# Moving k's turn one slot sooner and q's turn one slot later in a fused attention and expert kernel

## The chip, the cores and the metric

The kernel runs on one core of one Trainium2 chip. The metric is the device time in microseconds (us) of one execution. Four runs of the kernel before the change are shown, and one of them was profiled.

## The reference

Two stages are computed one after the other. The first is attention with a threshold, for 8 batches, 8 heads, 576 positions and head dimension 64. The second is a two-layer network over all 4608 rows, with a hidden width of 2048.

```
scores = (q @ k.T) / sqrt(64)
scores = where(scores >= rowmax(scores) - tau, scores, -1e9)     # tau = 0.02
attn   = exp(scores - rowmax);  attn /= rowsum(attn) + 1e-9
x      = (attn @ v), heads side by side                          # 4608 x 512
h      = x @ w_in                                                # 512 -> 2048
out    = (h - tanh(h)) @ w_out                                   # 2048 -> 512
```

Inputs and output are float32.

## The kernel before

**Tiles.** Two heads of one batch make a pair. There are 32 pairs, numbered 0 to 31, and four of them make a batch. A pair has 9 row tiles of 128 rows (`TPP`): tiles 0 to 3 are rows of the first head, tiles 5 to 8 of the second, and tile 4 ("M") holds the last 64 rows of both. There are 288 tiles in all.

**Slots.** One loop over `s` writes the order of all work by hand; each engine then executes its own instructions in that order. A step of this loop is called a slot here. In slot `s` the loop issues, in this order: `shift` (a small op on DVE that makes the bias `nb` from the row maxima) for tile s+7, `scores` for tile s+8 (`AHEAD` = 8), `kink` for tile s+5 (`MASK` = 5), `bend` (tanh on ACT of the hidden block of the slot before), `weights` of tile s (exp on ACT), one step of the two-layer network where there is one, `shrink` (DVE, `g`), stores, `attend` and `norm` for tiles of two slots before, `emit_x`, and at the end the steps that `plan` has for this slot. For pairs 0 to 3 `weights` and `attend` run four slots sooner.

**One tile.** `scores` (L327, and L317 for tile 4) multiplies qT with kT and with kS into one of two psum buffers of the pool `ps_big`. DVE copies this out with a scale and a row maximum (`sc`, L337), which frees the buffer. ACT masks it (`z`, L374). For pairs 0 to 5 PE transposes z (`psZ`, L394); from pair 6 on a DMA does it (`zT`, L382, on SP's queue). ACT takes the exponential (`pT`, L403 or L411), PE multiplies with v (`psO`, L440 and L429), and DVE normalises (L454, L455, L460). `emit_x` (L472, L478) transposes the result of a pair for the second stage.

**The second stage** of a batch is cut into steps of four matmuls: hidden steps (`psH`, L495, followed by tanh on ACT and `g` on DVE, L514) and output steps (`psY`, L521, followed by `yo` on DVE, L534). They are spread over slots of the following batch, beginning with its fifth slot, about one per slot.

**Preparing a pair.** Before pair p's first `scores` in slot `first` = 9p-8, these steps are put into `plan`:

```
PREP = ((LDK, load k), (LDK-1, load q), (LDK-2, load v),       # LDK = 16
        (8, split k), (7, split q), (5, turn k), (4, split_v))
```

A number d stands for slot `first` - d. `split` runs on POOL: three operations make a float16 high and low part (`khl` or `qhl`, L190 to L194). `turn` (L241) transposes nine 128x128 blocks on PE into a psum buffer of the same pool `ps_big` (`ps_k` or `ps_q`), and DVE copies them out (`kT` or `qT`, L264). For k, two copies on POOL then make `kS` (L270), with the halves exchanged. `split_v` runs on POOL after that. q's turn stands at d = 3, but for odd pairs from 9 on and for pair 30 (`q_by_dma`) it is a DMA transpose on SP's queue (L253) at d = 5. The weights are loaded in 16 pieces in the early slots, each followed by a cast on POOL (L628).

Since 9 slots make a pair, slot `first` - 5 is the slot in which the scores of the tile 4 of the pair before are issued.

Of the kernel before, what the change touches and what calls it, by code (L numbers as in the profile page):

```python
# [18 lines left out]
def kernel(  # L19
# [225 lines left out]
    def q_by_dma(p):  # L245

        return p >= 2 * HPAIR and (p % 2 == 1 or p == 30)

    def turn(p, t):
        hl = hls.pop((p, t))  # L250
        if t == "q" and q_by_dma(p):
            m = mats[p, t] = qk_pool.tile([P, W], FP16, name=f"{t}T", tag=t)
            nc.sync.dma_start_transpose(  # L253
                out=m.rearrange("p (c r) -> p c r", c=TPP),
                in_=hl.rearrange("p c a d -> p (c a d)"),
            )
            return
        ps = ps_big.tile([P, W], FP16, name=f"ps_{t}", tag="big")
        for c in range(TPP):
            turn_chunk(  # L260
                ps[:, c * P : (c + 1) * P], c, hl[:, c, :, :].rearrange("p a d -> p (a d)")
            )
        m = qk_pool.tile([P, W], FP16, name=f"{t}T", tag=t)
        nc.vector.tensor_copy(out=m, in_=ps)  # L264
        mats[p, t] = m
        if t == "k":
            sw = qk_pool.tile([P, W], FP16, name="kS", tag="ks")
            for lo, hi in ((0, D), (D, 0)):
                o, i = sw[lo : lo + D, :], m[hi : hi + D, :]
                nc.gpsimd.tensor_copy(out=o, in_=i)  # L270
            mats[p, "ks"] = sw
# [383 lines left out]
    for p in range(1, NPAIR):  # L655
        first = TPP * p - AHEAD
        for d, f in PREP[3 if p == 1 else 0 :]:
            d -= p == 1 and d in (3, 5)
            plan.setdefault(first - d, []).append(lambda p=p, f=f: f(p))
        d = 5 if q_by_dma(p) else 3 - (p == 1)  # L660
        plan.setdefault(first - d, []).append(lambda p=p: turn(p, "q"))

    load(0, "v")
# [27 lines left out]
    for s in range(-AHEAD, NTILE + LAG + 3):  # L691
        p, j = divmod(max(s, 0), TPP)
# [107 lines left out]
```

## Time and profile before

| what | value |
| --- | --- |
| median of four runs | 538.06 us (537.02 to 538.35) |
| the profiled execution | 538.18 us, of which the span of the instructions is 536.4 us |
| granted TensorE clock | 1.00 |
| busy: PE, DVE, ACT, POOL | 513.1, 427.4, 438.2, 290.9 us |
| scores copies `sc` on DVE (L337) | 288 of 0.752 us |
| k copies `kT` on DVE (L264) | 31 of 0.756 us |
| q copies `qT` on DVE (L264) | 18 of 0.752 us |
| `kS` copies on POOL (L270) | 62 of 1.143 us |
| q turns by DMA (L253) | 13, median 3.3 us from issue to landing |

PE is TensorE, DVE VectorE, ACT ScalarE, POOL GpSimd, and SP the queue that issues most DMAs. Matmuls are pipelined, so one that is listed with 0.379 us may be followed by the next much sooner, and a busy PE row is not PE at its peak. In the lines of the timeline the columns are: start, duration, engine, line, operation, output<-input, shapes and count, and in brackets the idle time before it with what ended it. The one who ended a wait is inferred, and where the engine named had long been done it was another.

### The profile page before, as it was taken

To read this page: it belongs to the slowest core of one execution; us is meant where nothing else is said; L and a number is where in the kernel's file an instruction comes from. 1 tells how busy PE (TensorE), PEld (TensorE's weight loads), DVE (VectorE), ACT (ScalarE), POOL (GpSimd) and SP (SyncE) were. 2 spreads that over 40 slices of the span, in tenths; PEclk is the share of its full clock that TensorE was granted. 3 is DMA by queue.
4 is the path that set the end of the run, shared out by engine and by line. 5 is a ranking of instruction groups with operands and counts; after the bars stand their busy time and mean duration, and the time that the engine had idled before them with its cause. 6 is when DMAs were issued, how large, how long until landed. Compare 5 with 4: busy or idle time off the path is not lost.

```text
span 536.4 us, 13042 instructions
## 1 busy us (share of the span) xinstructions
PE 513.1 (96%) x4782; PEld 287.9 (54%) x4782; DVE 427.4 (80%) x1202; ACT 438.2 (82%) x630; POOL 290.9 (54%) x390
## 2 busy tenths in 40 slices
PE   8989899998999999999999999999999999999997
PEld 4666565554555555555555555555555455444444
DVE  5889878988888988889888988898888888554440
ACT  5999888998898989899888989898989989543330
POOL 7999995766555666657555755566665720000000
PEclk9999999999999999999999999999999999999999
DMA  7555656998997988799988999889979885401113
GB/s 207 178 185 145 207 165 137 183 204 155 184 200 171 174 198 188 167 183 177 201 190 179 190 182 191 168 179 195 188 165 182 188 151 113 104 21 39 39 41 78
DMA packets 204768, 85.76 MB, mean 160 GB/s; under 512 B 172320, under 2 KB 197152, under 8 KB 204704
## 3 DMA queue, kind: packets, MB, share of 16 engines
q1 hardware_dynamic: 204112, 84.51, 73.8%
q8 instruction: 37, 0.61, 0.5%
q10 hardware_dynamic: 592, 0.43, 0.3%
q14 instruction: 27, 0.22, 0.1%
HBM read 36.70 MB, written 9.44 MB: 86 GB/s over the span
## 4 chain that ended last, share of the span: by engine, by line
PE 69%; DVE 16%; POOL 7%; ACT 3%; issue 3%; DMA 1%; SPq 0%; DVEq 0%; POOLq 0%; ACTq 0%
PE psY L521 21%; PE psH L495 18%; PE psS L327 14%; DVE sc L337 7%; PE psO L440 5%; DVE g L514 3%; PE psS L317 3%; PE psHt L495 3%; PE ps_k L241 2%; DVE kT L264 2%; ACT pT L403 2%; POOL kS L270 2%; DVE yo L534 1%; ACT z L374 1%; POOL w_in_sb L628 1%
## 5 line engine op out<-in xcount | busy, mean ns | idle before, releaser
L337 DVE TENSOR_SCALAR_CACHE_REDUCE sc<-psS 128x576 f32<-128x576 f32 x288 | 216.0, 752 | 23.2 <-PE psS L327 14.3
L374 ACT ACTIVATE z<-sc,nb 128x576 bf16<-128x576 f32 x256 | 193.5, 769 | 19.5 <-DVE nb L354 19.4
L521 PE MATMUL psY<-w_out_sb,g 128*128 128x512 bf16 (+1 forms) x592 | 146.0, 374 | 0.8 <-DVE yo L534 0.8
L411 ACT ACTIVATE pT<-zT 128x1152 f16<-128x1152 bf16 (+1 forms) x130 | 138.9, 1069 | 2.0 <-DMA zT<-z 2.0
L270 POOL COPY kS<-kT 64x1152 f16<-64x1152 f16 x62 | 70.8, 1143 | 128.2 <-DVE nb L354 126.6
L495 PE MATMUL psH<-xT,w_in_sb 128*128 128x512 bf16 x480 | 124.0, 379 | 2.3 <-DVE g L514 2.3
L327 PE MATMUL psS<-kT,qT 128*128 128x512 f16 (+1 forms) x512 | 104.4, 285 | 7.8 <-DVE sc L337 3.7
L508 ACT ACTIVATE th<-psH 128x512 f32<-128x512 f32 x128 | 75.5, 589 | 36.7 <-PE psH L495 35.5
L327 PEld LDWEIGHTS <-qT 128*128 128x128 f16 x1024 | 72.4, 97 | 57.8 <-issue 10.0
L514 DVE SCALAR_TENSOR_TENSOR g<-th,psH 128x512 bf16<-128x512 f32 x128 | 87.3, 682 | 18.7 <-ACT th L508 18.7
L327 PE MATMUL psS<-kS,qT 128*128 128x512 f16 x496 | 101.3, 286 | 0.9 <-POOL kS L270 0.7
L521 PEld LDWEIGHTS <-g 128*128 128x128 bf16 x592 | 50.7, 98 | 56.9 <-issue 4.0
L495 PEld LDWEIGHTS <-w_in_sb 128*128 128x128 bf16 x576 | 49.2, 98 | 58.2 <-issue 4.5
L440 PEld LDWEIGHTS <-pT 128*128 128x128 f16 x1280 | 55.7, 98 | 25.2 <-issue 1.9
L440 PE MATMUL psO<-vb,pT 128*128 128x65 bf16 x1280 | 61.2, 193 | 0.0
L194 POOL TENSOR_TENSOR khl<-kraw,khl 128x576 f16<-128x576 f32 x31 | 39.7, 1282 | 2.6
L194 POOL TENSOR_TENSOR qhl<-qraw,qhl 128x576 f16<-128x576 f32 x31 | 39.7, 1281 | 2.6
L403 ACT ACTIVATE pT<-psZ 128x640 f16<-128x640 bf16 (+1 forms) x54 | 35.5, 659 | 5.8 <-PE psZ L394 5.6
L264 DVE COPY kT<-ps_k 128x1152 f16<-128x1152 f16 x31 | 23.4, 756 | 14.1 <-PE ps_k L241 14.1
L534 DVE COPY yo<-psY 128x512 f32<-128x512 f32 (+1 forms) x31 | 21.1, 682 | 13.1 <-PE psY L521 11.1
L455 DVE TENSOR_TENSOR osb<-psO,rc 128x256 bf16<-128x256 f32 x64 | 27.2, 424 | 2.2
L354 DVE TENSOR_SCALAR nb<-mx 128x6 f32<-128x6 f32 (+1 forms) x160 | 24.4, 153 | 2.3
(81 smaller groups left out, 508.8 us busy)
## 6 DMA issues: line engine op xcount, KB each, us to landing
vraw<-in_v_dram SPq DMA_DIRECT2D x32, 256.0 KB, 3.5
out_dram<-yo SPq DMA_DIRECT2D x32, 256.0 KB, 2.8
kraw<-in_k_dram SPq DMA_DIRECT2D x31, 256.0 KB, 3.1
qraw<-in_q_dram SPq DMA_DIRECT2D x31, 256.0 KB, 3.7
wt<-in_moe_w_in_dram SPq DMA_DIRECT2D x8, 512.0 KB, 4.5
wt<-in_moe_w_out_dram SPq DMA_DIRECT2D x8, 512.0 KB, 4.6
zT<-z SPq DMA_TRANSPOSE x104, 3.5
kraw<-in_k_dram SPq DMA_DIRECT2D x32, 32.0 KB, 3.0
```

The lines of the kernel that those rows point to most:

```text
L194: nc.gpsimd.tensor_tensor(out=hl[:, :, 1, :], in0=x, in1=hl[:, :, 0, :], op=ALU.subtract)
L270: nc.gpsimd.tensor_copy(out=o, in_=i)
L327: nc.tensor.matmul(out=ps[:, dst], lhsT=lhs, rhs=kk[:, src], start=(n == 0), stop=(n == 1),)
L337: nc.vector.tensor_scalar(out=sc, in0=ps[:, lo : lo + S], scalar1=SC, scalar2=None, op0=ALU.mult, op1=ALU.max, accum_out=mx[:, c : c + 1],)
L374: nc.scalar.activation(out=z, in_=sc, func=ACT.Prelu, bias=nb, scale=1.0, alpha=STEEP)
L403: nc.scalar.activation(out=pt[:, off * P : (off + n) * P], in_=ps[:, 0 : n * P], func=ACT.Exp)
L411: nc.scalar.activation(out=pt[:, 0 : n * P], in_=zts.pop(i)[:, 0:n, :], func=ACT.Exp)
L440: nc.tensor.matmul(out=po[:, (j - 1 - 5 * hh) + ab, :], lhsT=pt[:, blk * P : (blk + 1) * P], rhs=vb[:, hh, c, :], start=(n == 0), stop=(n ...
L495: nc.tensor.matmul(out=ps, lhsT=w_in_sb[:, c, n * P : (n + 1) * P], rhs=xs[m][:, c, :] if m < B else xR[:, c, :, :], start=(c == 0), stop= ...
L508: nc.scalar.activation(out=th, in_=ps, func=ACT.Tanh)
L514: nc.vector.scalar_tensor_tensor(out=gs[m][:, n, :], in0=th, scalar=-1.0, in1=ps, op0=ALU.mult, op1=ALU.add,)
L521: nc.tensor.matmul(out=ps, lhsT=gs[m][:, n, ms * P : (ms + 1) * P], rhs=w_out_sb[:, n, cols], start=(n == 0), stop=(n == DF_C - 1),)
```

## The change

From pair 5 on, k's turn is put into slot `first` - 6 instead of `first` - 5. From pair 5 on, q's turn is put into slot `first` - 2 instead of `first` - 3 where PE does it; where a DMA does it (d = 5) it stays. Pair 4, the first of the second batch, and the pairs before it keep their slots. Nothing else is edited.

```diff
         for d, f in PREP[3 if p == 1 else 0 :]:
             d -= p == 1 and d in (3, 5)
+            if d == 5 and p >= 5:
+                d = 6
             plan.setdefault(first - d, []).append(lambda p=p, f=f: f(p))
-        d = 5 if q_by_dma(p) else 3 - (p == 1)
+        d = 5 if q_by_dma(p) else (2) if p >= 5 else 3 - (p == 1)
         plan.setdefault(first - d, []).append(lambda p=p: turn(p, "q"))
```

## The prediction

> **What bounds the kernel now.** I read the page's busy shares first, then busy time by stretch, then the waits of PE, then the order of events around the turns of single pairs. A slot is one step of the main loop. F stands for slot 9p-8, in which pair p's first score block is issued; F-6 is six slots earlier. Here are the page's busy line, and the stretches with their columns.
>
> ```profile
> PE 513.1 (96%) x4782; PEld 287.9 (54%) x4782; DVE 427.4 (80%) x1202; ACT 438.2 (82%) x630; POOL 290.9 (54%) x390
> ```
> ```profile
> core 0: us, PE busy (x) PEld busy (x) DVE busy (x) ACT busy (x) POOL busy (x), PEclk, DMA share, GB/s
> 55.00:78.00 23.00, 19.98 (x235) 13.05 (x234) 19.17 (x57) 19.55 (x32) 21.81 (x27) 1.00 0.56 181
> 78.00:94.00 16.00, 14.68 (x171) 9.56 (x169) 12.83 (x35) 13.98 (x24) 10.05 (x13) 1.00 0.69 150
> 107.40:135.00 27.60, 25.14 (x253) 14.25 (x252) 23.85 (x72) 25.03 (x35) 18.49 (x25) 1.00 0.90 182
> ...
> 165.60:223.60 58.00, 57.32 (x544) 31.91 (x543) 51.32 (x149) 52.33 (x73) 34.58 (x45) 1.00 0.85 184
> ```
>
> The last line is one batch of four pairs in the steady part: PE idles 0.68 us of 58. Four 512-column matmuls take 1.03 us and one alone 0.379, so each further one adds 0.217 us, and they follow one another at that step. The steady part is therefore bound by PE's own work, which the change doesn't alter. From 55 to 135 us it is different: PE idles 3.0, 1.3 and 2.5 us in the stretches shown, and POOL is busy for 21.8 of the first 23. This is where the moved turns can gain or lose.
>
> The Trainium skill (Perfetto Trace Analysis, Identifying the Most-Contended Engine) says that matmul busy time tells little about the distance to the roofline and that weight-load busy time and FLOPs should be used. By its 54% (287.9 us of 536.4) the steady part would look nearly half empty; the estimate by that page is that moved turns could shift the end by tens of us either way. Since the matmuls' starts already lie back to back, I go by the starts.
>
> ```profile
> PE psS L327 <- DVE sc L337: 3.7, 13, 0.8
> PE ps_q L241 <- POOL qhl L194: 1.9, 4, 1.0
> PE psZ L394 <- ACT pT L403: 1.3, 5, 0.3
> PE psS L327 <- DMA qT<-qhl: 1.2, 1, 1.2
> ```
>
> In PE's waits (total, times, longest), no turn costs more than a few us in the whole run. That caps the gain: the moves can't return more than the waits near them.
>
> **The change, part by part.** No instruction is added or removed. For 27 pairs (5 to 31) k's nine transposes (9 x 0.055 = 0.5 us of PE), its 0.756 us copy on DVE and its two 1.143 us copies on POOL are issued at the end of slot F-6 instead of F-5. For 14 pairs (5, 6, 7 and the even ones from 8 to 28) q's nine transposes and 0.752 us copy go from the end of F-3 to the end of F-2. The other q turns go by DMA and keep their place, so SP's order is unchanged. On POOL only one thing moves: in pair 5 the kS copies now precede a 1.04 us weight cast. The cast ends 2.4 us later, and SP's next weight load with pair 7's k load behind it waits for it (issued near 64.3 instead of 61.9). Pair 7's split starts at 77.4, so 10 us cover a 3.1 us load: nothing.
>
> *Pair 5.* POOL ends khl at 57.71.
>
> ```profile
> 56.58 0.48 PE L440 MATMUL psO<-vb,pT 128*128 128x65 bf16 x10
> 57.76 0.68 PE L241 MATMUL ps_k<-ident_f,khl 128*128 128x128 f16 x9
> 60.50 0.68 PE L241 MATMUL ps_q<-ident_f,qhl 128*128 128x128 f16 x9 [0.42 <-POOL qhl L194]
> 63.87 0.41 PE L327 MATMUL psS<-kS,qT 128*128 128x512 f16 x2 [0.30 <-POOL kS L270]
> ```
>
> Moved, k's turn stands right after that psO (issued out by 56.9) and waits until 57.76: 0.85 us in place of the 0.27 us that it waits now. The tile-4 scores queue behind it. The kT copy ends near 59.3 and F-4 needs its psum buffer: 59.34 for 58.63. q's turn no longer waits for qhl (0.59 us) but for sc of F-3, near 62.2; qT is ready near 63.7, just where F now waits for kS (ready near 62.8 instead). F's second half runs at 64.0 for 63.87. ACT, which is busy without a break from 64.6 to 71, starts its pT about 0.5 us later: I take +0.5 us, between 0 and +0.9 (the whole displacement of F-4 and more).
>
> *Pair 6.* khl ends at 68.93 and k's turn would be ready at 68.6 with pair 5's delay: it waits 0.4 us, but this swallows most of that delay. F-4 is late by 0.7. Then q's turn is gone from F-3, where F-2 now waits 0.43 us for DVE: F-2 runs at 74.4 for 74.88. F comes at 77.6 for 77.68. Net after pair 6: -0.1 us.
>
> *Pair 7.* khl is 3 us early. F-2 waits 0.82 us (90.77) because q's buffer waits behind norm, sc and g on DVE; moved, F-2 starts near 89.1. But q's turn then ends near 92.3, the qT copy near 93.1, and F needs it: 93.16 for 93.20. A gain of 1.7 us is given back at F. DVE keeps about 0.2 us of it.
>
> *Pairs 8 and 9.* DVE runs without a break from 101 to 112 us, and the same operations only change places: F-1's 0.46 us wait for the qT copy becomes a 0.35 us wait for sc. I take 0 for pair 8, and +0.1 for pair 9, whose tile-4 scores wait about 0.5 us for DVE in place of the 0.30 us at 116.42.
>
> *Pair 10* is the one real gain.
>
> ```profile
> 128.33 0.69 DVE L514 SCALAR_TENSOR_TENSOR g<-th,psH 128x512 bf16<-128x512 f32 x1 [1.22 <-ACT th L508]
> 128.93 0.75 DVE L264 COPY kT<-ps_k 128x1152 f16<-128x1152 f16 x1
> 129.73 0.41 PE L327 MATMUL psS<-kT,qT 128*128 128x512 f16 x2 [0.90 <-DVE nb L354]
> ```
>
> The kT copy is queued behind a g that waits 1.22 us for ACT's tanh, and F-3's scores wait for the buffer that this copy frees. Moved, the copy stands before that g and ends near 126.1; F-3 waits for sc only and starts near 128.7, 1.0 us earlier. F-2's 0.21 us wait goes too. What is late next: pair 11's qT by DMA. Pair 11's F (149.91) already waits 0.22 us for it, and SP issues it behind a zT that waits for ACT; ACT runs unbroken from 124.7 to 141.5 and comes forward by about 0.5 us only. I keep -0.5 (from 0 to -1.2).
>
> *The steady pairs, 11 to 31.* Cover, not gain, is what matters here. khl is ready 2 to 7 us before even the new place. Odd pairs: yo, then g, then the kT copy end 0.1 to 0.2 us before F-4 needs the buffer (pair 19: g ends 258.82, copy 259.57, F-4 issues at 259.72). Pairs 14, 18 and so on: k's turn fills PE until 358.59 (pair 26), and the tile-4 scores' buffer comes free at 358.58. q, even pairs: the turn ends about 0.17 us after its last start, the copy takes 0.75, and F comes 1.35 us (scores 0.49 plus a layer step 0.87) after the turn: a margin of 0.3 us. The nb of tiles 2 and 3 now stands behind the kT copy and ACT's z waits 0.7 to 0.9 us longer for it; ACT has idle time of 0.4 to 1.3 us just before or after (392.57: 0.78). I take 0, between -0.3 and +3 (below).
>
> The Trainium skill (Perfetto Trace Analysis, Optimization Strategy) says that a gap that repeats can mean too few buffers for the next tile. By that rule the two "big" buffers stay as scarce as they were, the moves cure nothing, and the sum is 0. The pair-10 rows show one gap that comes from queue order.
>
> Sum: +0.5 - 0.6 - 0.2 + 0.1 - 0.5 = -0.7 us, rounded to -0.6, since gains ahead of a resynchronising wait tend to be lost. The profiled execution took 538.18 us with a span of 536.4 (1.8 outside it, unchanged) and stands 0.12 above the median of 538.06. I forecast from the median: 537.5.
>
> **The rivals.** *Faster: the stalls between 56 and 135 us go for good.* The waits at the moved places, 0.59 (pair 5), 0.60 (6), 0.98 (7), 0.46 (8), 1.06 and 0.37 (10), are 4.1 us; less 1.4 for the new khl waits and their echo, 2.7 us remain: 535.4. For it: ACT and DVE have about 15% idle in these stretches. Against it: in pairs 5 and 7 F needs qT at once.
>
> *Slower: qT comes too late at F in the steady even pairs.* The margin is 0.3 us. A 0.60 us g between sc and the qT copy turns it into a wait of 0.3 us; over ten pairs (10, 12, ... 28) that is 3.0 us: 541.1. It decides once the copy starts over 0.3 us after the turn's end. Against it: in the changed order sc of F-2 stands directly before the qT copy in these pairs. For it: kT and qT copies now start 0.1 to 0.4 us after their turn, so margins of 0.1 to 0.3 are thin everywhere.
>
> *It does nothing to the steady part and the early terms cancel:* 538.1; this lies inside my forecast's range.
>
> **How the numbers follow.** This kernel's measurement tells about 0.2% (1.1 us) from no change. Within it, 0.43: the forecast's own range of 537.0 to 538.9 (pair 10 kept whole; pair 5 at its worst). Faster, 0.30: the first rival, or a part of it with pair 10 kept whole. Slower, 0.27: the second rival, or thin margins missed by 0.1 us in the 21 steady pairs (+2.1). The range for 8 in 10 is 535.6 to 540.4: nearly all of the faster case, and the slower one up to 2.3 us.
>
> **What would show it.** Right: ps_k waits for khl in pairs 5 and 6 of 0.4 to 0.9 us; the 1.06 us gap near 129.7 gone; PE busy in a steady batch still 57.3 of 58. Wrong: a wait of PE's scores for qT (or kT) that recurs in every even (or odd) pair, or a batch that is longer or shorter than 58.0 by over 0.2 us.

## The result: 0.2% faster, most of it in a part that was forecast to give nothing

The changed kernel takes 535.97 us (median of 36 runs, 534.62 to 537.04) against 537.12 us of the kernel before on the same chip (58 runs, 535.88 to 538.4). The ratio is 0.9977, with an interval of 0.9973 to 0.9982: by the ratio 1.24 us faster (1.0 to 1.5). That lies just over the 0.2% that count as a change here. The forecast was 537.5 us in a range of 535.6 to 540.4, with no change as the likeliest outcome. It was worked from 538.06 us, the median of the first four runs; 0.94 of the 1.53 us between forecast and measured time lie in the lower median that 58 runs give for the kernel before.

The two profiled executions are further apart: spans of 533.7 and 536.4 us. The profiled execution of before was one of its longer ones (538.18 us, 1.1 above the median just given), so the traces overstate the gain about twofold. They are used below for where things moved, and the times for how much it is worth.

From the page after, the busy line; and PE's busy time by stretch, with the columns of the table before (us, busy and instructions of each engine, clock, DMA share, GB/s):

```profile
PE 511.9 (96%) x4782; PEld 290.1 (54%) x4782; DVE 427.7 (80%) x1202; ACT 438.4 (82%) x630; POOL 291.0 (55%) x390
```
```profile
55.00:78.00 23.00, 19.50 (x233) 12.91 (x232) 18.91 (x56) 19.46 (x32) 21.75 (x28) 1.00 0.55 178
78.00:94.00 16.00, 15.05 (x171) 9.70 (x170) 13.62 (x40) 15.15 (x25) 9.95 (x12) 1.00 0.68 150
107.40:135.00 27.60, 25.29 (x256) 14.60 (x255) 24.11 (x74) 25.85 (x36) 19.94 (x26) 1.00 0.98 175
165.60:223.60 58.00, 57.41 (x548) 32.31 (x546) 51.57 (x147) 52.58 (x73) 34.78 (x45) 1.00 0.85 184
```

No engine does other work than before. Pair 5's stretch lost 0.5 us of PE's busy time, the next one won 0.4, the third (with pair 10) 0.15. The steady stretch shows 57.41 for 57.32, which looks like nothing. A busy share can't resolve what happened there; the starts of PE's instructions can. This table gives how much sooner (-) the first scores F of a pair start in the trace after than in the trace before, counted from pair 4, the last that the change doesn't touch:

| pair | 5 | 6 | 7 | 8 | 9 | 10 | 11 | 12 | 29 | 30 | end |
| --- | --- | --- | --- | --- | --- | --- | --- | --- | --- | --- | --- |
| us | +0.89 | +0.24 | +0.05 | -0.25 | +1.02 | -0.81 | -1.03 | -1.04 | -1.96 | -2.46 | -2.46 |

From pair 12 to pair 29, in the part forecast at 0, another 0.92 us is gained. It comes in equal steps of 0.21 us, at pairs 14, 18, 22 and 26 (the 0.09 at 27 is a wait of before for a qT by DMA): every steady batch takes 57.75 us instead of 57.96.

The waits of PE after, in total, times and longest:

```profile
PE psS L327 <- DVE sc L337: 2.4, 9, 0.4
PE psS L327 <- DMA qT<-qhl: 1.8, 2, 1.0
PE ps_q L241 <- POOL qhl L194: 1.5, 3, 1.0
...
PE ps_k L241 <- POOL khl L194: 0.7, 1, 0.7
```

The waits of the scores for `sc` fell from 3.7 to 2.4 us. The wait for a qT that a DMA brings rose from 1.2 to 1.8, and the forecast wait for khl is there once, in pair 5.

On the page the group of the kT copies points at DVE (busy, mean ns | idle of DVE just before, and what ended it). It is shown for before, then after:

```profile
L264 DVE COPY kT<-ps_k 128x1152 f16<-128x1152 f16 x31 | 23.4, 756 | 14.1 <-PE ps_k L241 14.1
```
```profile
L264 DVE COPY kT<-ps_k 128x1152 f16<-128x1152 f16 x31 | 23.4, 756 | 7.2 <-PE ps_k L241 6.8
```

DVE used to stand idle for 14.1 us in front of these copies, waiting for k's turn, and now only for 7.2 us. The row before was in the page that the forecast was made from, and the forecast does not use it. It is a pointer and not a price, since most of that idle time went to another place: in front of the qT copies it rose by about as much. The waits of DVE, before, then after:

```profile
DVE qT L264 <- PE ps_q L241: 0.7, 1, 0.7
```
```profile
DVE qT L264 <- PE ps_q L241: 7.3, 12, 0.7
```

What counts is which wait is passed on to PE.

### Where a steady batch wins 0.21 us

There are two places. The first is the joint of two batches, where for a few slots PE has no step of the second stage between two scores. Here it is before, around F of pair 25 (start, duration, engine, line, operation, tiles):

```profile
348.45 0.76 DVE L264 COPY kT<-ps_k 128x1152 f16<-128x1152 f16 x1 [1.09 <-PE ps_k L241]
...
353.04 0.68 DVE L514 SCALAR_TENSOR_TENSOR g<-th,psH 128x512 bf16<-128x512 f32 x1
...
353.34 0.41 PE L327 MATMUL psS<-kT,qT 128*128 128x512 f16 x2
...
353.64 0.75 DVE L337 TENSOR_SCALAR_CACHE_REDUCE sc<-psS 128x576 f32<-128x576 f32 x1
...
354.45 0.41 PE L327 MATMUL psS<-kT,qT 128*128 128x512 f16 x2
```

And after:

```profile
344.72 0.76 DVE L264 COPY kT<-ps_k 128x1152 f16<-128x1152 f16 x1
...
347.04 0.76 DVE L337 TENSOR_SCALAR_CACHE_REDUCE sc<-psS 128x576 f32<-128x576 f32 x1 [0.64 <-PE psS L327]
...
351.50 0.41 PE L327 MATMUL psS<-kT,qT 128*128 128x512 f16 x2
351.70 0.76 DVE L337 TENSOR_SCALAR_CACHE_REDUCE sc<-psS 128x576 f32<-128x576 f32 x1 [0.30 <-PE psS L327]
...
352.52 0.41 PE L327 MATMUL psS<-kT,qT 128*128 128x512 f16 x2
```

Before, DVE idles 1.09 us for k's turn and is then behind. The `sc` at 353.64 belongs to the scores before F and starts late, straight after the `g` at 353.04; the scores after F (354.45) need the buffer that it frees, and start 1.11 us after F (353.34). After, the kT copy (344.72) starts without a wait, and DVE is ahead: it waits for scores (0.64 us at 347.04), and the same `sc` (351.70) has waited 0.30 us for its scores, so it starts as soon as it can, and the distance is 1.02 us (351.50 to 352.52). That is 0.09 us.

The second place is q's turn in pairs 14, 18, 22 and 26. Before, in pair 26:

```profile
360.39 0.68 DVE L514 SCALAR_TENSOR_TENSOR g<-th,psH 128x512 bf16<-128x512 f32 x1
...
360.98 0.75 DVE L264 COPY kT<-ps_k 128x1152 f16<-128x1152 f16 x1
...
363.21 0.74 DVE L337 TENSOR_SCALAR_CACHE_REDUCE sc<-psS 128x576 f32<-128x576 f32 x1
...
363.40 0.67 PE L241 MATMUL ps_q<-ident_f,qhl 128*128 128x128 f16 x9
...
364.01 0.41 PE L327 MATMUL psS<-kT,qT 128*128 128x512 f16 x2
```

After:

```profile
363.14 0.67 PE L241 MATMUL ps_q<-ident_f,qhl 128*128 128x128 f16 x9
363.64 0.41 PE L327 MATMUL psS<-kT,qT 128*128 128x512 f16 x2
363.84 0.76 DVE L264 COPY qT<-ps_q 128x1152 f16<-128x1152 f16 x1 [0.60 <-PE ps_q L241]
...
364.99 0.41 PE L327 MATMUL psS<-kT,qT 128*128 128x512 f16 x2
```

Before, kT stood behind `yo` and `g`, DVE ran late, and the scores after q's turn started 0.61 us after it instead of 0.50: they waited 0.11 us for the buffer that the `sc` at 363.21 frees. After, the distance is 0.50. Both waits are shorter than a matmul is listed with (0.379 us), so they hide in the busy time of the row.

### The profile page after: what moved, and what is told of

Its sections match the earlier page's. It is cut to its first block, busy times and chain, and to the rows that moved or that the text cites. A ratio compares the mean times of both kernels' runs of the same rounds, so it can differ in the third digit from the quotient of the medians.

```text
span 533.7 us, 13053 instructions
## 1 busy us (share of the span) xinstructions
PE 511.9 (96%) x4782; PEld 290.1 (54%) x4782; DVE 427.7 (80%) x1202; ACT 438.4 (82%) x630; POOL 291.0 (55%) x390
## 4 chain that ended last, share of the span: by engine, by line
PE 75%; POOL 8%; DVE 6%; DMA 4%; ACT 3%; issue 2%; SPq 1%; POOLq 0%; DVEq 0%; ACTq 0%
PE psY L521 23%; PE psH L495 19%; PE psS L327 16%; PE psO L440 5%; PE psS L317 3%; DVE sc L337 3%; PE psHt L495 3%; PE ps_k L241 2%; POOL kS L270 2%; DMA qT<-qhl 2%; POOL w_in_sb L628 1%; PE psO L429 1%; PE ps_q L241 1%; DVE g L514 1%; DVE yo L534 1%
```

## The experiments

All are edits of the two lines that the change touches. The diffs of `k_only`, `q_only` and `dma_only` are taken against the kernel before, the others against the changed kernel, and they show only the lines that differ. Runs with a ratio were timed beside the kernel before on the same chip. In this table "steady" is the length of a steady batch in the trace, "F waits" the sum of what F waits for a qT by DMA over the odd pairs from 9 on and pair 30, and "pair 12" and "end" are shifts as in the table above.

| kernel | ratio | steady | F waits | pair 12 | end |
| --- | --- | --- | --- | --- | --- |
| before, and the profile again | | 57.96, 57.96 | 1.7, 2.1 | 0, +0.11 | 0, -0.16 |
| the change | 0.9977 [0.9973, 0.9982] | 57.75 | 2.1 | -1.04 | -2.46 |
| k_only | 0.9978 [0.9969, 0.9988] | 57.75 | 1.9 | -1.69 | -1.63 |
| q_only | 0.9964 [0.9952, 0.9977] | 57.86 | 1.9 | -1.80 | -2.80 |
| early_only | 1.0007 [0.9995, 1.0019] | 57.97 | 1.8 | -1.15 | -1.62 |
| late_only | 0.9982 [0.9973, 0.9992] | 57.75 | 2.2 | -0.72 | -0.99 |
| q_two | 1.0221 [1.0207, 1.0235] | 59.80 | 1.8 | +3.68 | +11.51 |
| qdma6 | 0.9938 [0.9924, 0.9951] | 57.75 | 0 | -1.82 | -4.22 |
| best | 0.9925 [0.9911, 0.9939] | 57.75 | 0 | -2.41 | -4.81 |
| dma_only | 0.9977 [0.9967, 0.9987] | 57.96 | 0 | -1.57 | -3.04 |
| early_dma | 0.9960 [0.9947, 0.9972] | 57.96 | 0 | -1.83 | -3.29 |

Single executions scatter: `late_only` is the kernel before up to F of pair 10, and its trace stands 0.48 us sooner there and 0.72 at pair 12 all the same. Shifts at pair 12 and at the end carry that uncertainty; the steady batch, which repeats within 0.01 us but for single waits such as that of `k_only` in pair 22, does not.

**k_only**: k's turn sooner, q's left in its place.

```diff
+            if d == 5 and p >= 5:
+                d = 6
```

> Only k's turn is moved (pairs 5 to 31); q's turn keeps its slot. Theory A (both moves gain by shortening waits in the steady part, 0.1 us a batch each, and k's also ends the wait in pair 10): a steady batch takes 57.88 us (before 57.98, both moves 57.75), the gap of about 1 us in pair 10 is gone, and the time is 0.9980 to 0.9988 of before. Theory B (all of the gain lies before 150 us, as the forecast had it): a steady batch takes 57.98 us and the time is 0.9985 to 0.9995. Theory C (the difference of the two profiles is mostly chance in when the q transposes by DMA land): the time is within 0.9995 to 1.0005.

Measured: 0.9978, with a steady batch of 57.75 us. k's move alone gives the whole step of 0.21 us, where half of it (57.88 us) had been expected. Its trace gives much of this back later in single waits: 0.52 us after q's turn in pair 22, and 0.76 and 1.15 us at F of pairs 27 and 30 for a qT by DMA.

**q_only**: q's turn later, k's left in its place.

```diff
-        d = 5 if q_by_dma(p) else 3 - (p == 1)
+        d = 5 if q_by_dma(p) else (2) if p >= 5 else 3 - (p == 1)
```

> Only q's turn is moved (pairs 5, 6, 7 and the even ones from 8 to 28); k's turn keeps its slot. Theory A: a steady batch takes 57.87 us (the 0.11 us wait of the scores after q's turn in pairs 14, 18 and so on is gone, the wait at the joint of two batches stays), the gap in pair 10 stays, and the time is 0.9985 to 0.9998 of before. Theory B: a steady batch takes 57.98 us, time 0.9995 to 1.0010. Theory C: the same as B.

Measured: 0.9964, with a steady batch of 57.86 us. q's move gives half of the step: with q later, the second place (q's turn in every fourth pair) has no wait, while the joint keeps its 1.11 us. The two moves overlap; they do not add (0.21 and 0.10, together 0.21).

The time is another matter: 0.9964 is 1.9 us (1.2 to 2.6), far beyond the 0.9985 to 0.9998 expected and no worse than the whole change (0.9977). The steady batches give 0.4 us of it. The rest lies elsewhere: in its trace F is 0.40 us sooner in pair 6, 0.75 in pair 8 and 1.80 in pair 12, and pair 10's gap, which was expected to stay, is gone. How much of that the edit causes was not settled, since a single execution scatters by 0.7 us there.

**early_only** and **late_only**: both moves, for pairs 5 to 10 only, and for pairs 11 and up only.

```diff
-            if d == 5 and p >= 5:
+            if d == 5 and 5 <= p <= 10:
```
```diff
-            if d == 5 and p >= 5:
+            if d == 5 and p >= 11:
```

(with the same condition in the line for q)

> Both turns are moved for pairs 5 to 10 only. Theory A: a steady batch takes 57.98 us, as before, and the time is 0.9985 to 0.9995 of before (pair 10's 1.0 us, less what pairs 5 and 6 lose to the wait for khl). Theory B: the whole gain, 0.9973 to 0.9982. Theory C: 0.9995 to 1.0010.

> Both turns are moved for pairs 11 to 31 only. Theory A: a steady batch takes 57.75 us and the time is 0.9975 to 0.9985 of before (0.2 us in each of five to six batches, and up to 0.4 us less wait for pair 30's q transpose). Theory B: a steady batch takes 57.98 us and the time is 0.9995 to 1.0005. Theory C: as B.

Measured: 1.0007 and 0.9982. The steady pairs carry the gain (0.97 us, between 0.4 and 1.5; the trace gives 0.92 between pairs 12 and 29, in `late_only` as in the changed kernel). `early_only` keeps the batch of before, and its time is that of the expectation by which the early gain is chance. The six early pairs with both moves, in which the forecast saw all that was to be won or lost, give nothing that the times show: between 0.3 us of gain and 1.0 us of loss. The one trace of `early_only` has pair 12 sooner by 1.15 us, but that execution took 536.31 us and was among the shortest of its kernel (median 537.61).

**before_2**: the kernel before, profiled once more.

> The kernel before once more, for a second profile. Theory C' (where the early waits fall is chance of one execution): pair 10's wait of 1.06 and 0.37 us and the F waits of pairs 9, 11, 27 and 30 come out differently by 0.5 us or more in all, while a steady batch takes 57.98 us again. If the pair-10 wait is fixed by the queue order, it is again 1.0 to 1.4 us.

Measured: 538.17 us. The gap in front of pair 10's F-3 is there again (0.91 us, before 1.06, and 0.37 in front of F-2 in both), as expected if the order of the queues makes it. The waits of F for a qT by DMA are not the same: 0.30, 0.51, 0.12, 0.46 and 0.71 us in pairs 9, 11, 25, 27 and 30, where the first trace has 0.22, 0.09 and 1.38 in pairs 11, 27 and 30. Those waits vary from one execution to the next by up to 0.7 us each, which is more than the effect of a steady batch.

**qdma6**: the change, with the DMA transposes of q issued one slot sooner.

```diff
-        d = 5 if q_by_dma(p) else (2) if p >= 5 else 3 - (p == 1)
+        d = 6 if q_by_dma(p) else (2) if p >= 5 else 3 - (p == 1)
```

> Both turns moved as in the change, and the q transposes by DMA (odd pairs from 9, pair 30) are issued one slot sooner too, in slot F-6. In the profiles so far the F scores of pairs 9, 11, 27 and 30 wait between 1.7 and 2.2 us in all for a transposed q. Theory D (these waits are what keeps the early gain out of the times): they fall under 0.8 us in all, a steady batch stays at 57.75 us, and the time is 0.9945 to 0.9965 of before. Theory E (SP's queue and the DMA engines are full there, so a sooner q transpose only delays the z transposes behind it): ACT's wait for zT grows by about what F's wait falls, and the time is 0.9970 to 0.9990.

Measured: 0.9938, a little better than the 0.9945 to 0.9965 expected, and F never waits for such a qT. ACT's wait for zT, which by the other theory would have grown, is 0.3 us in all (0.7 in the changed kernel). In pair 30 the changed kernel issues it and waits for it as follows:

```profile
419.00 1.56 SPq L253 DMA_TRANSPOSE qT<-qhl  x1
...
423.22 0.42 PE L327 MATMUL psS<-kT,qT 128*128 128x512 f16 x2 [0.82 <-DMA qT<-qhl]
```

In `qdma6` the same scores find it there:

```profile
414.38 1.64 SPq L253 DMA_TRANSPOSE qT<-qhl  x1
...
421.15 0.41 PE L327 MATMUL psS<-kT,qT 128*128 128x512 f16 x2
```

From issue to use it is 4.2 us in the first, with a wait, and 6.8 in the second, without one. The gain is more than the 1.6 us of one slot (57.75 us for 36), because on SP's queue the transpose now stands ahead of two loads of q, a zT and a store instead of behind them.

**q_two**: the change, with q's turn one slot later still.

```diff
-        d = 5 if q_by_dma(p) else (2) if p >= 5 else 3 - (p == 1)
+        d = 5 if q_by_dma(p) else (1) if p >= 5 else 3 - (p == 1)
```

> k's turn as in the change, q's turn two slots later than before, at the end of slot F-1, so that F's scores stand right behind it on PE. If the forecast's margin of 0.3 us (a layer step and scores, 1.35 us, less 0.17 us latency, 0.75 us copy and semaphores) is what hides the qT copy, then nothing hides it here: F waits about 1.0 us in each even pair, a steady batch takes about 59.8 us (57.75 plus two such waits) and the time is 1.014 to 1.022 of before. If PE had hidden slack, a batch would stay under 58.5 us and the time under 1.008.

Measured: 1.0221 and 59.80 us a batch, both as expected, the time at the edge of its range. This is the slower rival with its point passed: qT's copy comes after F is due, in every even pair. The chain of turn, copy and F in the trace of `q_two`, pair 26:

```profile
375.82 0.67 PE L241 MATMUL ps_q<-ident_f,qhl 128*128 128x128 f16 x9
...
376.53 0.76 DVE L264 COPY qT<-ps_q 128x1152 f16<-128x1152 f16 x1
377.34 0.42 PE L327 MATMUL psS<-kT,qT 128*128 128x512 f16 x2 [0.85 <-DVE nb L354]
```

The scores start at the end of the qT copy (377.29). The trace names `nb`, which had long been done; what ends the wait is the copy. So the margin of 0.3 us that the forecast relied on is used up by one slot more, which costs 2.05 us a batch.

**best**: q's turns from pair 5, k's from pair 7, q's DMA transposes one slot sooner.

```diff
-            if d == 5 and p >= 5:
+            if d == 5 and p >= 7:
```

(beside the edit of `qdma6`)

> q's turn moved from pair 5, k's turn only from pair 7 (so that it doesn't wait for khl in pairs 5 and 6), and the q transposes by DMA one slot sooner. Theory A (steady gain by k and q, loss by khl in pairs 5 and 6): pair 6's F comes 0.4 us sooner than in the profile of before, as with q moved alone, a steady batch takes 57.75 us; with D the time is 0.9940 to 0.9960 of before, with E 0.9965 to 0.9980.

Measured: 0.9925, 533.44 us against 537.48, better than the 0.9940 to 0.9960 expected. F of pair 6 is 0.39 us sooner, as expected. Leaving out k's move in pairs 5 and 6 takes away the loss of the wait for khl in pair 5: in the traces pair 5 stands at -0.01 us for +0.86 in `qdma6`, and pair 12 at -2.41 for -1.82. Of the kernels run here it is the fastest, though its interval overlaps that of `qdma6`.

**dma_only** and **early_dma**: before, and `early_only`, each with q's DMA transposes one slot sooner. They were to tell whether the early moves are worth something once F no longer waits.

```diff
-        d = 5 if q_by_dma(p) else 3 - (p == 1)
+        d = 6 if q_by_dma(p) else 3 - (p == 1)
```

> The kernel before with one edit: every transpose of q by DMA is issued in slot F-6 instead of F-5; no turn by TensorE moves. Steady batch 57.95 to 58.0 as before. All theories: F's waits for a qT brought by DMA (2.1 us summed in the profile taken again of before) are gone, and pair 10's gap before F-3 stays at 0.6 to 1.1 us. Theory D (the early moves are worth something, but give it back at these F): a ratio of 0.9960 to 0.9985 here, and early_dma lower by 0.0015 to 0.0025 (0.8 to 1.4 us). Theory E (the early moves are worth nothing by themselves): the same ratio here and early_dma equal within 0.0008.

> The change for pairs 5 to 10 only, and in all pairs the transposes of q by DMA in slot F-6. Steady batch 57.95 to 58.0 as before. Theory D: no F waits for a qT brought by DMA, pair 10's gap is gone and its 1.0 us is kept to the end, so that the ratio is 0.0015 to 0.0025 below that of dma_only. Theory E: equal to dma_only within 0.0008, since pair 5's and pair 6's losses or a later wait take what pair 10 gains.

Measured: 0.9977 and 0.9960. One part of both expectations failed: pair 10's gap, which I expected to stay in `dma_only` at 0.6 to 1.1 us, is gone there (0 before F-3, 0.12 before F-2), although no turn on PE was moved. The chain behind that gap therefore goes further back than the forecast followed it. Before:

```profile
119.32 3.29 SPq L382 DMA_TRANSPOSE zT<-z  x1
...
124.69 1.16 ACT L411 ACTIVATE pT<-zT 128x1152 f16<-128x1152 bf16 x1 [1.82 <-DMA zT<-z]
...
127.72 0.57 ACT L508 ACTIVATE th<-psH 128x512 f32<-128x512 f32 x1
128.33 0.69 DVE L514 SCALAR_TENSOR_TENSOR g<-th,psH 128x512 bf16<-128x512 f32 x1 [1.22 <-ACT th L508]
```

And in `dma_only`:

```profile
118.52 1.59 SPq L382 DMA_TRANSPOSE zT<-z  x1
...
122.75 1.16 ACT L411 ACTIVATE pT<-zT 128x1152 f16<-128x1152 bf16 x1 [0.40 <-DMA zT<-z]
...
125.78 0.58 ACT L508 ACTIVATE th<-psH 128x512 f32<-128x512 f32 x1
126.50 0.68 DVE L514 SCALAR_TENSOR_TENSOR g<-th,psH 128x512 bf16<-128x512 f32 x1
```

ACT waits 1.82 us for a zT, its tanh is late by that, `g` waits for the tanh, and kT waits for `g`. Where that first wait is 1.3 us or more and kT stands behind `g`, the gap is there (before 1.06, `before_2` 0.91, `late_only` 0.57, with waits of 1.82, 1.66 and 1.32). In `q_only`, whose kT still stands behind `g`, the wait is 0.95 and there is no gap. So a shorter wait at the source closes the gap. Whether the order on DVE closes it too, with a long wait at the source, is not shown: in every trace with k's turn moved in pair 10 that wait was short (0.69 us in the changed kernel, 0.66 in `k_only`, 0.87 in `early_only`, 1.00 in `early_dma`, less in the rest).

Between the two theories the times do not decide. `early_dma` is lower by 0.0017, within what the first of them (the early moves are worth something) expects, and its median by 0.5 us, but the intervals overlap. In the traces the difference is 0.26 us at pair 12. The early moves are worth between nothing and about half a microsecond with those waits gone; a closer figure stays open.

## Why the prediction was near, and where it was wrong

**The steady pairs: the step that failed.** The forecast took 0, between -0.3 and +3, on the ground that PE's scores follow one another at their own step. The runs show -0.92 us between pairs 12 and 29 (-0.83 without pair 27's DMA wait), outside that bound, and `late_only` puts it into the times. The error was in reading 0.68 us of idle time a batch as PE's floor, and in asking of each moved copy only whether it would still be in time (cover) and not whether its old place cost something. It cost twice a batch: at the joint DVE idled 1.09 us for k's turn and was late for the next `sc`, and in every fourth pair the kT copy stood behind `yo` and `g` and made a later `sc` late. Each made PE wait about 0.1 us for a buffer, too short to appear in PE's waits, from which the forecast took its cap on the gain. The sign that the prediction named for being wrong, a batch that differs from 58.0 by over 0.2 us, is the one that appeared: 57.75.

**Steady margins: right.** qT's copy ends near 364.6 in pair 26 and F starts at 364.99, 0.4 us later, where a margin of 0.3 had been forecast; no wait of F for a copied qT recurs in the even pairs. The forecast longer waits of ACT for `nb` are there:

```profile
L374 ACT ACTIVATE z<-sc,nb 128x576 bf16<-128x576 f32 x256 | 193.8, 769 | 30.6 <-DVE nb L354 30.3
```

They were 19.5 us before; 11 us more of ACT's waiting did not keep the batch from getting shorter.

**Pair 5: +0.5 forecast, +0.89 in the trace (+0.84 to +0.88 in the four others that move its k), near the upper end of 0 to +0.9.** The wait for khl was foreseen (0.85 us forecast):

```profile
57.60 0.68 PE L241 MATMUL ps_k<-ident_f,khl 128*128 128x128 f16 x9 [0.71 <-POOL khl L194]
```

What was mis-sized is how much of it F catches up: almost nothing. **Pair 6**: the net was forecast at -0.1 and is +0.24; k's turn starts at 68.81, right when khl is ready, where a wait of 0.4 us had been forecast to swallow the delay. **Pair 7**: right. F does wait for the qT copy, and the gain is given back there:

```profile
93.07 0.42 PE L327 MATMUL psS<-kT,qT 128*128 128x512 f16 x2 [0.36 <-DVE qT L264]
```

It was forecast at 93.16. The step from pair 6 to pair 7 is -0.19 us, as forecast (-0.2). **Pair 8**: 0 forecast, -0.3.

**Pairs 9 and 10: the gap is gone, but not shown to be for the reason given; what came late next is right in kind.** The forecast had the kT copy's place behind `g` as the reason. In the trace after, ACT's wait at the source is 0.69 us instead of 1.82, a length at which `q_only` has no gap although its kT stands behind `g`. The reason stays open. The forecast kept half of the gain, because a qT by DMA would be late next. One is, but in pair 9, where the forecast had pair 11:

```profile
120.78 0.42 PE L327 MATMUL psS<-kT,qT 128*128 128x512 f16 x2 [1.00 <-DMA qT<-qhl]
```

Taken together, the early terms were forecast at -0.6. The times give +0.4 with bounds of -0.3 and +1.0 (`early_only`). So it is luck that the total came near (-0.6 forecast, -1.24 measured): a gain that was expected early, and that the times do not show, stood in for one that came late.

**The rivals.** The faster one had the right sign for another reason: it put the gain between 56 and 135 us. The slower one was sound in its mechanism, as `q_two` shows, with its point one slot away.

**The notes on the chip.** The Trainium skill (Perfetto Trace Analysis, Optimization Strategy) takes a gap that repeats as a possible sign of too few buffers for the next tile. The two repeating waits here were indeed waits for one of the two "big" buffers, but with the buffers unchanged they went when DVE emptied them in another order: 57.96 to 57.75 us a batch. The page says only that it can mean this; the sum of 0 that the forecast drew from it does not hold in this case. The weight-load share that the same page uses for PE (Identifying the Most-Contended Engine) is 54% before and after and showed neither the bound nor the change, and the tens of us that the forecast drew from it are far from the 1.24 measured.

## What to carry to other kernels

When an engine executes in program order, ask of an instruction that is moved what its old place cost the engine it runs on. Idle time in front of it can become a backlog that another engine waits for some slots later: here 1.09 us of it at the joint became a wait of 0.09. The sum of such idle time does not give the price (7 us less before kT, as much more before qT, 0.21 us a batch won); the start of the instruction that is held up does. Where a stretch repeats, compare starts over one period in hundredths of a microsecond, since a wait of 0.1 us a batch is invisible in a busy share and makes most of the result here. Follow a gap back until its chain ends, and before crediting the gain look at all transfers that run with a margin of a few tenths: a transfer put one slot sooner (0.2% by itself) brought the changed kernel from 0.9977 to 0.9938.

## What the runs showed of the hardware

When a qT by DMA arrived varied enough between executions of one kernel to move single waits by up to 0.7 us: F of pair 30 waited 1.38 us in one execution of the kernel before and 0.71 in the other, with the same instructions and order. The transpose itself took as long from issue to landing (3.46 and 3.51 us); SP came to it 10.96 and 10.24 us after F of pair 29. On the queue before it stands a load of q (L151), whose issue took 1.98 us in the first and 0.59 in the second. The trace of one execution can therefore mislead about an effect of 1.2 us (58 executions of the kernel before spread over 2.5), while the steady batch repeated within 0.01 us in both. Issuing one and the same zT on SP's queue took 3.29 us in the kernel before (the row at 119.32) and 2.91 in its second execution, 1.38 in the changed kernel, whose order on that queue is the same, and 1.59 in `dma_only` (the row at 118.52). What holds the queue for the longer time was not tried.
